# Projecting Q and K of the first two tiles from centred tokens, and scaling them afterwards on GpSimd

## The chip, the cores and the metric

The kernel runs on one core of a Trainium2 chip. The metric is the device time of one execution in microseconds (us); the smaller the better. Times of several runs are given as a median with the lowest and the highest.

## The reference

A block on 2048 tokens of 640 features, in bf16. The tokens are normalised (`_layernorm`, no weights), and two branches read the result: attention over a short dilated window, with 32 heads of 20 features, and a gated product of two linear layers. Both are added to the tokens.

```python
m = jnp.mean(x, -1); v = jnp.var(x, -1)
xn = (x - m) / jnp.sqrt(v + 1e-5)
q, k, v = (xn @ wqkv)                       # 640 x 1920, 32 heads of 20
idx = pos[:, None] - 2 * arange(8)[None]    # 8 keys, each second token back
attn = softmax(where(idx >= 0, q . k[idx] * 20 ** -0.5, -1e9))
A = (sum over w of attn * v[idx]) @ wo
B = ((xn @ w_gate) * (xn @ w_up)) @ w_down  # 640 -> 1536 -> 640
out = x + A + B
```

The deviation is one number for each token, so it may be divided out before or after the projection: `((x - m) * r) @ W` equals `((x - m) @ W) * r`.

## The kernel before

The tokens lie in 16 tiles of 128 (`XST`, one tile is 128 partitions by 640). For each tile, `front(t)` takes statistics on VectorE (two `bn_stats` of 320 columns at L579, `bn_aggr` at L582 into `MV`), the root of the variance on ScalarE (L589) and its reciprocal on VectorE (L596), both into `SD`, and then the normalised tokens `XNS`: on VectorE for tiles 0 to 5 (L608 in two pieces for tiles 0 and 1, L611 for the others), on ScalarE from tile 6 on (L614). The projections need the features on the partitions, so each tile is turned into `XNT`: tiles 0 to 3 by TensorE against an identity (L646) with a copy out of PSUM (L656, L658, L665), tiles 4 to 15 by a transposing DMA from SP's queue (L679).

Q and K of tiles 0 and 1 are projected by `proj_group` in `spread` (L734): for each chunk of 128 input features, five products of 128 by 128 into two neighbouring banks of PSUM, so that work can begin when the first chunks of the tokens and of the weights are there. ScalarE copies the result out (L707) into `QT` and `KT`. All other Q, K and V projections go by `mms` (L702). V of the first 512 tokens (`proj_v(0, m)`) needs tiles 0 to 3 in `XNT` and V's weights.

Before the first transposes, TensorE runs nine fillers of 512 columns on constants, and after tile 0's transposes three of 256 (`warm`, L686).

Behind the projections come: products of Q with shifted K on VectorE (`products`, L885 and L934), their sums by head on TensorE (L1017), softmax, the weighted V (L1196 on VectorE, L1201 on GpSimd, sums by head on TensorE at L1255), the gated layer (L1319) and the output projections (L1420, L1471).

The order on each engine is fixed when the program is built. `Sched.run` holds a list of tasks with priorities and estimated durations and times (`occ`, `land`), and picks the next one; at run time each engine goes through its list in order and waits for semaphores. Some instructions of VectorE and GpSimd carry `lock`: those of the one engine wait until those of the other, placed before them, are done. So an estimate that changes can move any instruction after it. The order of the first loads is written out by hand; the rest of SP's queue comes from `loads()`, in its order:

```python
x_half(0, 2.85)
x_half(1, 3.25, eng="act")
x_load(1, land=4.2)
wqkv_load(0, 0, 3, eng="act", land=5.5)
wqkv_load(1, 0, 2, land=6.4)
wqkv_load(0, 3, NCH, land=7.2)
x_load(2, land=7.6)
wqkv_load(1, 2, NCH, land=9.0)
```

After these, `loads()` issues tiles 3 to 11, V's weights in one transfer and tiles 12 to 15, each of these last once its place in `XST` is free.

Of the kernel before, what the change touches and what calls it, by code (L numbers as in the profile page):

```python
# [357 lines left out]
def build_kernel(nc, A_x, A_wqkv, A_wo, B_x, B_w_gate, B_w_up, B_w_down, out):  # L358
# [67 lines left out]
    QUAD = {2: (1, 0), 3: (1, 0)}  # L426
    LAST_DMA = ()
# [11 lines left out]
    MV = sb("MV", [128, NT, 2], FP32)  # L439
    SD = sb("SD", [128, NT, 4], FP32)  # L440
# [8 lines left out]
    vscr = nc.dram_tensor("v_scratch", [D, PAD + S], BF16, kind="Internal").ap()  # L449

# [53 lines left out]
    COPY = (("act", "act"), ("dve", "act"))  # L504
    STEPS = (((0, 2), (2, 3), (3, 4), (4, NCH)), ((0, 2), (2, 3), (3, NCH)))
# [19 lines left out]

    def loads():
        def t(f, *a):
            return Task("sp", lambda: f(*a), prio=0)

        for t_ in range(3, NXS):  # L530
            yield t(x_load, t_)
        yield t(wqkv_load, 2)
        for t_ in range(NXS, NT):
            yield have("apply", t_ - NXS)
            yield t(x_load, t_)

        def w(T, src):
            dma(T[:], src.rearrange("(c p) n -> p c n", p=128), w=[T[:]], name="ld_w")

        def pads():  # L540
            z = ZERO[:, 0:PAD].unsqueeze(1).to_broadcast([128, NCH, PAD])
            dma(vscr[:, 0:PAD].rearrange("(c p) s -> p c s", p=128), z, r=[ZERO[:, 0:PAD]], w=[("vscr", "pad")], name="vpad")

        yield have("xnt", NT - 1)
        yield t(w, WG, B_w_gate)
        yield t(pads)
        yield t(w, WU, B_w_up)

        def copy_x():
            a, b = ohbm[0:3 * JB, :], xhbm[0:3 * JB, :]  # L550
            o, i = a.rearrange("(p r) n -> p (r n)", p=128), b.rearrange("(p r) n -> p (r n)", p=128)
            op("sp", lambda e: e.dma_start(o, i), w=[("outx",)], dma=True, name="outx", nbytes=2e6)

        yield num(2, "lg")
        yield t(copy_x)
# [15 lines left out]
    def front(t):  # L571
        x, st = XST[:, xslot(t), :], STATS[:, t, 0:12]
        xs, mv = XNS[:, t % NXN, :], MV[:, t, 0:2]
        sd, rstd, nmr = SD[:, t, 0:1], SD[:, t, 1:2], SD[:, t, 2:3]
# [12 lines left out]
        def sqrt():  # L587
            o, i = SD[:, t0:t1, 0:1], MV[:, t0:t1, 1:2]
            op("act", lambda e: e.activation(o, i, ACT.Sqrt, bias=EPSC[:, 0:1]), r=[("mv", k) for k in ts] + [EPSC[:]],  # L589
               w=[("sd", k) for k in ts], name=f"sd{t}", occ=0.36)  # L590
            for k in ts:
                mark("sd", k)

        def recip():
            o, i = SD[:, t0:t1, 1:2], SD[:, t0:t1, 0:1]
            op("dve", lambda e: e.reciprocal(o, i), r=[("sd", k) for k in ts], w=[("rstd", k) for k in ts], name=f"rstd{t}", occ=0.16)  # L596
            if t >= N_DVE_A:
                n, m = SD[:, t0:t1, 2:3], MV[:, t0:t1, 0:1]
                op("dve", lambda e: e.scalar_tensor_tensor(n, m, -1.0, o, op0=ALU.mult, op1=ALU.mult),
                   r=[x for k in ts for x in (("mv", k), ("rstd", k))], w=[("nmr", k) for k in ts], name=f"nmr{t}", occ=0.13)  # L600
# [3 lines left out]
        def apply():  # L604
            if t < N_SPLIT:
                for a, b in [(128 * lo, 128 * hi) for lo, hi in PARTS[t]]:
                    o, i = XNS[:, t, a:b], x[:, a:b]
                    op("dve", (lambda o, i: lambda e: e.tensor_scalar(o, i, mv[:, 0:1], rstd, op0=ALU.subtract, op1=ALU.mult))(o, i),  # L608
                       r=[i, ("mv", t), ("rstd", t)], w=[o], name=f"lnap{t}", occ=0.09 + (b - a) * 0.55e-3)
            elif t < N_DVE_A:  # L610
                op("dve", lambda e: e.tensor_scalar(xs, x, mv[:, 0:1], rstd, op0=ALU.subtract, op1=ALU.mult),  # L611
                   r=[x, ("mv", t), ("rstd", t)], w=[xs], name=f"lnap{t}", occ=0.45)
# [6 lines left out]
        if t == 1:  # L619
            yield have("apply", 0)  # L620
        for i in range(2):
            if t == 2 and i == 0:
                yield have("apply", 1)
            if t == 2 and i == 1:
                yield have("xnt", t - 1)
# [11 lines left out]
        yield Task("dve" if t < N_DVE_A else "act", apply, r=[("rstd", t), x], w=[xs], prio=p)  # L637
        o = XNT[:, :, t * TS:(t + 1) * TS]
        if t < N_PE_T:
            hold = []  # L640

            def trans(k, *bs):
                hold.extend((b, PS[:, b, :].bitcast(BF16)[:, 0:NCH * 128].rearrange("p (c f) -> p c f", c=NCH)) for b in bs)
                for c in range(*PARTS[t][k]) if t < N_SPLIT else range(NCH):
                    i, q = xs[:, c * 128:(c + 1) * 128], hold[k][1][:, c, :]
                    op("pe", (lambda q, i: lambda e: e.transpose(q, i, IDENT[:]))(q, i), r=[i, IDENT[:]], w=[q],  # L646
                       name=f"tr{t}_{c}", occ=0.057, lat=0.2)
                if t == 0 and k:
                    warm(N_WARM)

            def part(k, eng):
                b, tpv = hold[k]
                lo, hi = PARTS[t][k]
                a, i = o[:, lo:hi], tpv[:, lo:hi]
                if eng == "dve":
                    X = op("dve", lambda e: e.tensor_copy(a, i), r=[PS[:, b, :]], w=[a], name=f"xntcp{t}_0", occ=0.1 + 0.08 * (hi - lo))  # L656
                else:
                    X = op("act", lambda e: e.activation(a, i, ACT.Copy), r=[PS[:, b, :]], w=[a], name=f"xntcp{t}_1",  # L658
                           occ=0.12 + 0.12 * (hi - lo))
                K.free_bank(b, X)  # L660
# [8 lines left out]

            if t < N_SPLIT:  # L670
                for k, ((lo, hi), e) in enumerate(zip(PARTS[t], COPY[t])):
                    yield Task("pe", (lambda k: lambda *bs: trans(k, *bs))(k), r=[xs[:, lo * 128:hi * 128]], prio=p, banks=1)
                    yield Task(e, (lambda k, e: lambda: part(k, e))(k, e), r=[PS[:, hold[k][0], :]], prio=p - 1)
            else:
                yield Task("pe", lambda b: trans(0, b), r=[xs], prio=p, banks=1)
                yield Task("dve" if t < N_DVE_C else "act", copy, r=[PS[:, hold[0][0], :]], prio=p)
        else:
# [3 lines left out]
            yield Task("sp", dmat, r=[xs], prio=1)  # L681
        mark("xnt", t)

# [36 lines left out]
    def proj_group(items, s0, n, prio, keys):  # L720
        hold = []

        def spread(k, *bs):
            which = items[0][0]
            if bs:
                p = PS[:, bs[0], :]
                p = bass.AP(p.tensor, p.offset, [p.ap[0], [n, NCH], [1, n]])
                hold.append((bs[0], [(qk_dst(which, 0, NCH, s0, n), p, NCH * n)]))
            b = hold[0][0]
            for c in range(*STEPS[s0 // TS][k]):  # L730
                for m in range(NCH):
                    o = PS[:, b + m // 4, m % 4 * n:m % 4 * n + n]
                    l, x = wcols(which, c, m), XNT[:, c, s0:s0 + n]
                    op("pe", (lambda o, l, x, c, m: lambda e: e.matmul(o, l, x, start=(c == 0 and m % 4 == 0), stop=(c == NCH - 1 and m >= 3)))(o, l, x, c, m),  # L734
                       r=[l, x], w=[o], name=f"p{which}_{s0}_{m}_{c}", occ=n / 2400 + 0.0024, lat=0.3)

# [10 lines left out]
        def ev():  # L747
            b, outs = hold[0]
            X = evac(outs, f"pev{items[0][0]}_{s0}")
            for i in range(2 if wide else 1):  # L750
                K.free_bank(b + i, X)
# [5 lines left out]
        wide = prio < 10  # L757
        if wide:
            for k, (lo, hi) in enumerate(STEPS[s0 // TS]):
                yield Task("pe", (lambda k: lambda *bs: spread(k, *bs))(k), r=[wcols(items[0][0], hi - 1, 0), XNT[:, hi - 1, s0:s0 + n]],  # L760
                           prio=prio, banks=0 if k else 2, contig=not k)
        else:
            yield Task("pe", go, r=[wcols(items[0][0], NCH - 1, 0), XNT[:, NCH - 1, s0 + n - TS:s0 + n]], prio=prio, banks=1)
        if wide:
            yield have("sd", 2 + items[0][0]) if s0 else have("xnt", 1)
        yield Task("act", ev, r=[o for _, o, _ in hold[0][1]], prio=5)

    def proj_qk():
        for pair in (0, 2):
            for t in (pair, pair + 1):  # L770
                yield have("xnt", t)
                for which in (0, 1):
                    K.spawn(proj_group([(which, 0, 4 if pair else 5)], t * TS, TS, 10 if pair else FIRST + 0.5 * which + 0.2 * t, None))
            if pair:
                for which in (0, 1):
                    K.spawn(proj_group([(which, 4, 1)], pair * TS, 2 * TS, 10.2, None))
# [12 lines left out]
    def proj_v(j, m):  # L789
# [15 lines left out]
        yield Task("pe", go, r=[WQKV[:, WPOS[2], 4, 0:64], XNT[:, NCH - 1, j * JB:(j + 1) * JB]], prio=30 + j, banks=1)  # L805
# [12 lines left out]
    free = list(range(NPR - 1))  # L818
# [693 lines left out]
    GROUPS = ((4, 5), (6, 7), (8, 9), (10, 11), (12, 13), (14, 15))  # L1512
    N_DVE_A = 6
    N_DVE_C = 5
    N_SPLIT = 2
    N_WARM = 3
# [9 lines left out]
    x_half(0, 2.85)  # L1526
    x_half(1, 3.25, eng="act")
    x_load(1, land=4.2)
    wqkv_load(0, 0, 3, eng="act", land=5.5)
    wqkv_load(1, 0, 2, land=6.4)  # L1530
    wqkv_load(0, 3, NCH, land=7.2)
    x_load(2, land=7.6)
    wqkv_load(1, 2, NCH, land=9.0)
    K.t["act"] = 2.95
# [10 lines left out]

    K.spawn(loads())
    for t in range(NT):
        K.spawn(front(t))
    K.spawn(proj_qk())
# [50 lines left out]
```

## Time and profile before

| | us |
|---|---|
| median of 3 runs | 264.64 (264.5 to 264.82) |
| the profiled execution | 264.51 |
| its span, first to last instruction | 262.8 |

| engine | busy us | share of the span | instructions |
|---|---|---|---|
| PE (TensorE matmul) | 259.3 | 99% | 1586 |
| DVE (VectorE) | 219.0 | 83% | 259 |
| POOL (GpSimd) | 160.5 | 61% | 97 |
| ACT (ScalarE) | 112.7 | 43% | 198 |

The profile shows one execution, in us from its first instruction. Its page gives the busy time of each engine, the chain of waits that ended last, the costliest groups of instructions (line, engine, operation, output<-inputs) and the transfers with the time from issue to landing. The trace behind it can be asked for the same in any stretch of time, for one line or one tile, and for who waited for whom. SP and ACT issue most transfers; a "q" behind an engine's name marks its sequencer.

### The profile page before, as it was taken

What the parts mean: (1) busy time and instruction counts of PE and PEld (TensorE: products, weight loads), DVE (VectorE), ACT (ScalarE), POOL (GpSimd) and SP (SyncE); (2) the same over time, 40 slices, a digit from 0 to 9 for tenths busy, and PEclk for the clock granted to TensorE, in tenths of its full rate; (3) what the DMA queues carried; (4) which work ended last, traced back from release to release, by engine and by line L of the source; (5) the groups of instructions that cost most, each with busy time, mean ns of one, the idle gap of its engine ahead of it and who ended that gap; (6) DMA issues with size and microseconds to landing.
All of it is one profiled execution on the core that took longest, in us unless ns stands there. A gap on an engine that the chain in (4) does not pass through costs nothing.

```text
span 262.8 us, 4098 instructions
## 1 busy us (share of the span) xinstructions
PE 259.3 (99%) x1586; PEld 135.7 (52%) x1586; DVE 219.0 (83%) x259; ACT 112.7 (43%) x198; POOL 160.5 (61%) x97
## 2 busy tenths in 40 slices
PE   8999999999999999999999999999999999999996
PEld 3986964444444444444444444444444444445675
DVE  4888899999897897868779899999989989995041
ACT  3559987546522121224267665451324116211300
POOL 3000000000699999899983465899979999999300
PEclk9999999999999999999999999999999999999999
DMA  7996699932489996640349702666679766821621
GB/s 222 365 216 106 119 183 386 336 152 100 127 153 190 248 207 118 118 87 1 80 118 302 171 7 50 142 131 174 148 181 199 189 140 143 140 60 37 91 65 50
DMA packets 47891, 39.77 MB, mean 151 GB/s; under 512 B 23776, under 2 KB 45536, under 8 KB 47840
## 3 DMA queue, kind: packets, MB, share of 16 engines
q1 hardware_dynamic: 44448, 32.72, 48.3%
q0 software_dynamic: 2736, 6.16, 13.8%
q10 hardware_dynamic: 688, 0.64, 0.7%
q8 instruction: 12, 0.20, 0.3%
q14 instruction: 7, 0.06, 0.1%
HBM read 25.07 MB, written 7.23 MB: 123 GB/s over the span
## 4 chain that ended last, share of the span: by engine, by line
PE 97%; DMA 1%; DVE 1%; ACT 0%; issue 0%
PE PS L1319 40%; PE PS L702 23%; PE PS L1420 21%; PE PS L1471 7%; PE PS L734 2%; PE PS L1017 2%; PE PS L1255 2%; DMA XST<-in_A_x_dram 1%; PE PS L646 1%; DVE STATS L579 0%; DVE XNS L608 0%; PE PS L686 0%; ACT SD L589 0%; DVE FB L1484 0%; DVE MV L582 0%
## 5 line engine op out<-in xcount | busy, mean ns | idle before, releaser
L1201 POOL TENSOR_TENSOR SV<-PV 128x1024 bf16<-128x1024 f32 x40 | 94.1, 2523 | 17.8 <-DVE SM L1050 4.2
L1196 DVE TENSOR_TENSOR PV<-VX,PS 128x1024 f32<-128x1024 bf16 (+1 forms) x54 | 90.7, 1730 | 2.8 <-POOL SV L1201 2.8
L702 PE MATMUL PS<-XNT,WQKV 128*128 128x512 bf16 (+2 forms) x390 | 60.7, 316 | 0.0
L1319 PE MATMUL PS<-XNT,WG 128*128 128x512 bf16 x240 | 59.7, 379 | 0.0
L1319 PE MATMUL PS<-XNT,WU 128*128 128x512 bf16 x240 | 59.6, 379 | 0.0
L702 PEld LDWEIGHTS PS<-XNT,WQKV 128*128 128x128 bf16 x390 | 37.8, 112 | 21.9 <-ACT LOG L1028 0.8
L934 DVE TENSOR_TENSOR PRF<-PS,KT 128x1024 f32<-128x1024 f32 x32 | 38.0, 1217 | 0.3 <-PE PS L702 0.3
L1319 PEld LDWEIGHTS PS<-XNT,WG 128*128 128x128 bf16 x240 | 23.3, 98 | 28.7 <-DVE XNT L1328 0.4
L1319 PEld LDWEIGHTS PS<-XNT,WU 128*128 128x128 bf16 x240 | 23.5, 98 | 28.3
L960 POOL TENSOR_TENSOR PRF<-PRF,PRF 128x1024 f32<-128x1024 f32 x8 | 21.0, 2629 | 21.6 <-DVE LOG L1077 21.6
L707 ACT ACTIVATE HT<-PS 128x512 bf16<-128x512 f32 x24 | 14.4, 598 | 35.4 <-PE PS L1319 35.4
L1420 PE MATMUL PS<-HT,WD 128*128 128x512 bf16 x120 | 27.5, 379 | 0.0
L885 DVE TENSOR_TENSOR PRD<-QT,KT 128x2048 bf16<-128x2048 bf16 x24 | 27.5, 1217 | 0.0
L707 ACT ACTIVATE UX<-PS 128x512 bf16<-128x512 f32 x15 | 9.0, 597 | 41.6 <-PE PS L1420 41.6
L1036 POOL MEMSET LOG<- 32x6 bf16 (+6 forms) x7 | 0.4, 95 | 42.1 <-ACT LOG L1028 42.1
L993 POOL TENSOR_TENSOR PRD<-PRF,PRF 128x1024 bf16<-128x1024 f32 x8 | 20.6, 2625 | 0.1
L971 POOL TENSOR_TENSOR PRF<-PRF,PRD 128x1024 f32<-128x1024 f32 x8 | 19.7, 2564 | 0.0
L1420 PEld LDWEIGHTS PS<-HT,WD 128*128 128x128 bf16 x120 | 11.6, 98 | 14.4 <-ACT OT L1264 0.4
L1420 PE MATMUL PS<-OT,WO 128*128 128x512 bf16 x75 | 18.6, 379 | 0.0
L1328 DVE TENSOR_TENSOR HT<-HT,PS 128x512 bf16<-128x512 bf16 x18 | 12.3, 684 | 7.2 <-PE PS L1319 7.1
L1484 DVE TENSOR_TENSOR FB<-PS,XR 128x320 bf16<-128x320 f32 (+2 forms) x9 | 4.1, 455 | 16.2 <-PE PS L1471 15.2
L579 DVE BATCH_NORM_STATS2 STATS<-XST 128x6 f32<-128x320 bf16 x32 | 14.2, 467 | 1.9 <-DMA XST<-in_A_x_dram 1.9
(76 smaller groups left out, 247.0 us busy)
## 6 DMA issues: line engine op xcount, KB each, us to landing
VX<-v_scratch SPq DMA_DIRECT2D x80, 130.0 KB, 3.1
PRF<-PRF POOLq DMA_DIRECT2D x8, 512.0 KB, 5.4
v_scratch<-VST SPq DMA_DIRECT2D x4, 640.0 KB, 6.1
XST<-in_A_x_dram SPq DMA_DIRECT2D x15, 160.0 KB, 5.6
WG<-in_B_w_gate_dram SPq DMA_DIRECT2D x1, 1920.0 KB, 9.0
WU<-in_B_w_up_dram SPq DMA_DIRECT2D x1, 1920.0 KB, 12.5
out_dram<-in_A_x_dram SPq DMA_DIRECT2D x1, 1920.0 KB, 17.9
WD<-in_B_w_down_dram SPq DMA_DIRECT2D x1, 1920.0 KB, 8.7
```

The lines of the kernel that those rows point to most:

```text
L702: op("pe", (lambda o, l, x, c, first: lambda e: e.matmul(o, l, x, start=first, stop=(c == NCH - 1)))(o, l, x, c, first), r=[l, x], w=[o], ...
L707: X = op("act", (lambda o, i: lambda e: e.activation(o, i, ACT.Copy))(o, i), r=[i], w=[o], name=name, occ=0.12 + n * 0.9e-3)
L885: op("dve", lambda e: e.tensor_tensor(s[:], qb, kv, ALU.mult), r=[q, rk], w=[s[:]], name=f"prod{j}_{r}_{c}", occ=1.15, lock=True)
L934: X = op("dve", lambda e: e.tensor_tensor(o[:], qb, kv, ALU.mult), r=[q, rk, ("qev", j, c)], w=[o[:]], name=f"prow{j}_{r}_{c}_{q0}", occ=1.17)
L960: yield Task("pool", lambda: op("pool", lambda e: e.tensor_tensor(x, x, y, ALU.add), r=[x, y] + tokens(), w=[x], name=name, occ=2.36, lock ...
L971: yield Task("pool", lambda: op("pool", lambda e: e.tensor_tensor(x, x, z, ALU.add), r=[x, z] + tokens(), w=[x], name=name + "c", occ=2.36 ...
L993: yield Task("pool", lambda: op("pool", lambda e: e.tensor_tensor(o, a, y, ALU.add), r=[a, y] + tokens(), w=[o], name=f"qend{j}_{r}_{q0}", ...
L1196: last[0] = op("dve", lambda e: e.tensor_tensor(p, vw, a, ALU.mult), r=[vv] + rk, w=[p], name=f"pv{u}_{x}_{r0}", occ=0.09 + 1.1 * nr)
L1201: X = op("pool", lambda e: e.tensor_tensor(o, p[:, :, 0, :], p[:, :, 1, :], ALU.add), r=[p[:]] + tokens(), w=[o], name=f"pva{u}_{x}", occ= ...
L1319: op("pe", (lambda l, x, c: lambda e: e.matmul(PS[:, b, :], l, x, start=(c == 0), stop=(c == NCH - 1)))(l, x, c), r=[l, x], w=[PS[:, b, :] ...
L1420: op("pe", (lambda l, x, i: lambda e: e.matmul(PS[:, b, :], l, x, start=(i == 0), stop=(i == n - 1)))(l, x, i), r=[l, x], w=[PS[:, b, :]], ...
L1471: op("pe", (lambda l, x, i: lambda e: e.matmul(dst, l, x, start=(i == 0), stop=(i == n - 1)))(l, x, i), r=[l, x], w=[PS[:, b, :]], name=f" ...
```

## The change

For tiles 0 and 1, a new thread `raw(t)` subtracts only the mean (`XCT`): tile 0 on VectorE with the mean of `bn_aggr`, tile 1 on ScalarE with a mean that ScalarE sums itself (`xsum`). TensorE turns these centred tokens, VectorE copies them to `XRAW`, and `raw_group` projects Q and K from them, chunk by chunk, into PSUM; ScalarE copies the results as fp32 to `RAW`. The reciprocal deviations of both tiles are stored to a scratch in DRAM and loaded again along the free dimension on all partitions (`ROWS`), and GpSimd multiplies, four times 128 by 640 (`rsc`). Statistics' root and reciprocal are taken for tiles 0 and 1 together; they are normalised too, later, by VectorE, and turned by a transposing DMA, since V and the gated layer read `XNT`. ScalarE's program has a second load of a function table, between tile 1's centring and the first root.

Q's weights and K's are loaded in chunks of 128 input features, Q's from two queues in turn; V's in two parts of columns. After K's weights the order on SP's queue is: the store of the reciprocals (which waits for them), tiles 4 to 6, the load of the rows (which waits for the store), the transposes of tiles 0 and 1 (each waits for the normalised tile), V's weights 0 to 255, tile 7, V's weights 256 to 639, tiles 8 to 11, and then as before. The list of free places for products begins with others (the first ones are taken by the new tiles), and the planner puts five more wide projections ahead of the first sums by head.

On TensorE the order is now: tile 0's transposes, fillers, Q of tile 0 (25 products), tile 1's transposes, 55 products of K and Q of tiles 0 and 1, tile 2's transposes, the 20 products left, and tile 2's and 3's work as before.

```diff
+    RAW = K.sbuf("RAW", [128, 2, 2, NCH, TS], FP32, a_wd)
+    XRAW = K.sbuf("XRAW", [128, NCH, 2 * TS], BF16, a_wd + 3 * 4096)
+    XCT = K.sbuf("XCT", [128, 2, D], BF16, a_pr)
+    XSUM = K.sbuf("XSUM", [128, D], FP32, a_pr + 4096)
+    ROWS = K.sbuf("ROWS", [128, 2 * TS, 2], FP32, a_wd + 4 * 4096)
...
     def loads():
...
-        for t_ in range(3, NXS):
-            yield t(x_load, t_)
-        yield t(wqkv_load, 2)
+        yield have("rstd", 1)
+        yield Task("sp", row_store, r=[("rstd", 1)], prio=0)
+        for t_ in range(4, 7):
+            yield t(x_load, t_, "sp", lands[t_])
+        yield Task("sp", row_load, r=[("rscr",)], prio=0)
+        for k in range(N_RAW):
+            yield have("xs", k)
+            mark("dtr", k)
+            yield have("xnt", k)
+        yield t(wv_load, 0, 256, 15.1)
+        yield t(x_load, 7, "sp", lands[7])
+        yield t(wv_load, 256, D, 16.6)
+        for t_ in range(8, NXS):
+            yield t(x_load, t_, "sp", lands[t_])
+        yield have("xnt", 5)
...
+    def raw(t):
...
+        def total():
+            op("act", lambda e: e.activation(XSUM[:], x, ACT.Copy, scale=-1.0 / D, accum_out=mean), ...)
...
+            if CENTRE[t] == "dve":
+                op("dve", lambda e: e.tensor_scalar(o, i, mean, None, op0=ALU.subtract), ...)
+            else:
+                op("act", lambda e: e.activation(o, i, ACT.Identity, bias=mean), ...)
...
+    def norm(which, t):
+        yield have("raw", which, t)
+        yield have("rows")
+        yield have("apply", 5)
...
+            op("pool", lambda e: e.tensor_tensor(d, x, rs, ALU.mult), ..., lock=True)
...
-    free = list(range(NPR - 1))
+    free = [6, 7, 8, 9, 10, 3, 4, 0, 1, 2, 5]
...
-    GROUPS = ((4, 5), (6, 7), (8, 9), (10, 11), (12, 13), (14, 15))
+    GROUPS = ((0, 1), (4, 5), (6, 7), (8, 9), (10, 11), (12, 13), (14, 15))
...
-    x_half(0, 2.85)
+    x_half(0, 3.05)
     x_half(1, 3.25, eng="act")
-    x_load(1, land=4.2)
-    wqkv_load(0, 0, 3, eng="act", land=5.5)
...
+    x_load(1, eng="act", land=3.9)
+    wqkv_load(0, 0, 1, land=4.5)
+    wqkv_load(0, 1, 2, eng="act", land=4.9)
+    wqkv_load(0, 2, 3, land=5.3)
+    wqkv_load(0, 3, 4, eng="act", land=5.7)
+    wqkv_load(0, 4, NCH, land=6.1)
+    wqkv_load(1, 0, 1, land=6.5)
+    x_load(2, land=6.95)
+    wqkv_load(1, 1, 2, land=7.4)
+    wqkv_load(1, 2, 3, land=7.8)
+    wqkv_load(1, 3, 4, land=8.2)
+    x_load(3, land=8.65)
+    wqkv_load(1, 4, NCH, land=9.1)
```

## The prediction

> **What bounds the kernel now.** I read the chain that ended last first, then who waits on TensorE (PE), then the first 14 us of that chain in order of time.
>
> ```profile
> PE 97%; DMA 1%; DVE 1%; ACT 0%; issue 0%
> ```
> ```profile
> PE PS L686 <- PEq L1585: 0.9, 1, 0.9
> PE PS L646 <- DVE XNS L608: 0.3, 1, 0.3
> ```
> PE is the path. After its first transposes it never waits again, so the time is "when useful PE work starts" plus a fixed amount of PE work plus any wait that the change adds. The start:
>
> ```profile
> 0.82 2.25 DMA XST<-in_A_x_dram
> ...
> 3.10 0.90 DVE STATS L579 x2
> ...
> 4.02 0.22 DVE MV L582
> ...
> 4.26 0.30 ACT SD L589
> ...
> 4.59 0.17 DVE SD L596
> ...
> 4.79 0.35 DVE XNS L608
> ...
> 5.19 0.29 PE PS L646 x2
> 5.48 0.00 issue
> 5.48 0.34 PE PS L646 x3
> 5.82 0.33 PE PS L686 x3
> 6.15 1.40 PE PS L734 x25
> ```
> The change takes the square root and reciprocal (4.26 to 4.79) out of this chain. What it adds lies on ScalarE (ACT), on SP's queue and in the landings of loads, for which I read the timeline, the DMA view and the page's queue rows:
>
> ```profile
> 39.95 0.60 ACT L707 ACTIVATE QT<-PS 128x512 bf16<-128x512 f32 x1 [0.48 <-PE PS L702]
> 40.56 1.28 ACT L1541 ACT_TABLE_LOAD   x1
> 41.86 1.08 ACT L707 ACTIVATE KT<-PS 128x512 bf16<-128x512 f32 x2
> ```
> ```profile
> L679 SPq DMA_TRANSPOSE XNT<-XNS x12: 1199/1274/2644, 16.4 to 33.2; - x12
> ```
> ```profile
> q8 instruction: 12, 0.20, 0.3%
> ```
> A table switch costs 1.3 us of ACT. A DMA transpose holds SP for 1.2 to 1.3 us, the first one for 2.64. The instruction queue moves 12 packets of 16 KB; its packet records show the first two at 13.39 (1.11 us long) and 17.26 (1.40 us). Each holds one DMA engine: the 800 KB V weights, at the rate of the loads around them (160 KB per 0.44 us: XST landings 10.23, 10.67, 11.12 ...), were due 2.2 us after 13.36 and landed at 16.76, 1.2 late; the transpose issued at 16.44 landed after 3.75 us, against 2.6 for most.
>
> **The change part by part.** Sums are against the profiled execution, 264.51 us (span 262.8, 1.7 around it), 0.13 below the median 264.64; I add the differences to the median.
>
> *Start, −0.54.* Aggregation ends at 4.23, so the centring pieces run at 4.26 and 4.52 (0.35, 0.37, the L608 rows). The last three transposes start at 4.95, not 5.48; three fillers follow as before; the first projection moves from 5.99 to 5.45. The copies out of PSUM go to VectorE (DVE): 0.29 for two chunks (L656), 0.37 for three (between that and 0.49 for five), ending 5.27 and 5.69; chunk 2 is needed at 5.45 + 10 × 0.056 = 6.01. Amounts of PE work stay: 20 transposes, 12 fillers, the same projections.
>
> *Weights by chunk, 0 to +0.3, taken 0.* By bytes in order of issue at 160 KB per 0.44 us from 320 KB at 4.40, Q's chunks land at 4.85, two by 5.7, two by 6.6; they are needed at 5.45, 5.73, 6.01, 6.29, 6.57. K's come last at 9.7 and are needed at 10.7. A wait here eats into the next one rather than adding to it.
>
> *Tile 1 on ACT, tile 2 behind it, 0 to +0.6, taken +0.1.* Tile 1 lands 4.4 to 4.85 (4.40 before). ACT then sums it (0.70 to 0.91, the 640-element rows L707 and L614), centres two pieces (0.38 to 0.51, 0.49 to 0.62, the L658 rows and the same with 0.13 of SBUF and pointer cost from L614), ending near 6.4, loads the square root's table (1.28) to 7.75 and takes the root (0.30) to 8.05. DVE stands in order behind it: reciprocal, two statistics, aggregation, root, reciprocal, tile 2's normalisation. In the trace that string takes 2.25 us from L579 at 7.97 to L646 at 10.21, so tile 2 is ready at 8.09 + 0.08 + 2.2 = 10.4. PE gets there after 25 + 5 + 55 instructions of 0.056 and two changeovers: 10.25.
>
> *Normalised tiles 0, 1 for V.* DVE gains two normalisations (0.45 each, L611) and three copies, loses 0.64 of tile 1's: about +1.2. DVE had 2.9 us of waits for the root's reciprocals in the front, so its products move by a microsecond or so; the first logits stand 45 and not 40 wide projections after the rest, +1.08 of cover: 0. If the cover is gone, it's that microsecond.
>
> *SP's queue, 0 to +2.0, taken +0.45.* Here work is moved. After the K load SP waits for the reciprocal, stores rows, loads x4 to x6, waits about 2 us for the store (ATX landings 1.9), loads the rows, waits for normalised tiles 0 and 1 (near 11.9 and 12.9), issues two transposes, and only then V's weights and x7 to x11, which in the kernel before were issued by 8.4. With 1.25 us a transpose the first V part (320 KB) is issued at 14.45 and lands at 17.0 to 17.3 (x loads: first data about 1 us after issue, 0.88 of data, 0.4 to 0.75 to landing); PE wants it at 17.5 (18.04 before, less 0.54). The second part (480 KB, behind x7) would land at 19.0, wanted at 17.5 + 10 × 0.216 = 19.7. But the second instruction packet stands 0.78 us ahead of V in PE's order (17.26 against 18.04), so near 16.8, and holds one engine to about 18.1; that engine then has 1.7 us of x7 and V left: 19.8, landed 20.2. Hence +0.45 between 0 and 0.7. If the first transpose takes 2.64 here too, everything behind moves by 1.4: the second rival.
>
> *GpSimd's four scalings, 0.* 2523 ns × 640/1024 = 1.6 us each, from tile 5's normalisation (17.6) to 24.1, the row transfer long landed. Who waits: DVE's first product, 29.57 before. Cover 5 us.
>
> *Later stages, 0.* Product slots are dealt out in another order; PE's amounts are equal. The tightest later cover is the last sums: GpSimd ends at 244.16, PE starts L1255 at 245.50.
>
> Sum: −0.54 + 0.1 + 0.45 = 0.0, so 264.6.
>
> **Two rules against the change.** The row of the table load above shows ACT running again 0.02 us after 1.28 us of loading, with nothing lost ahead of it. The Trainium skill, "ScalarE: Activation LUTs", section "What ACT_TABLE_LOAD costs", counts a drain of about 1.38 us besides, 2.66 in all; by an estimate from that page tile 2 would be ready 1.4 us later. This trace disagrees.
> The nine fillers run at 427 ns for 512 columns, the transposes at 5.19 follow each other at 56 ns for 128: the full rate came between 4.65 and 5.19 (the granted-clock record: 4.76). Work that starts at 4.7 has no margin. The Trainium skill, "TensorE: Matmul & The Clock Gate", section on the HAM clock gate, says the window that decides is free-running, so the change of rate may come later in another run; the three times of before, within 0.32 us, speak against much of that.
>
> **The rivals.**
> 1. *All hidden* (chance 0.17). V's weights and tile 2 come in time: 264.64 − 0.54 = 264.1. For it: every margin I gave is only a few tenths. Against: the loads behind the transposes.
> 2. *V's weights become the path* (0.30). If the first transpose holds SP for 2.64 us as in the trace, V's first part is issued at 15.85, lands at 18.7 free, 19.6 if the instruction packet holds one engine; PE, in order, waits 1.2 to 2.0: 265.3 to 266.1. It decides as soon as the landing passes 18.0, where the gain is gone. For: that row. Against: the long one was issued 0.8 us before the packet at 17.26, with an earlier load still queued on that engine; the transpose at 33.24, with a packet at 34.14, held SP 1.28 us. So it may be the packet, not being first.
> 3. *ACT stands still after the second table load* (0.06). If it stood as long again as the load's 1.28 us, tile 2 would be ready at 11.7, PE would wait 1.4 there, and V, wanted 1.4 later, no more: 264.64 − 0.54 + 1.4 = 265.5. It decides once tile 2 passes 10.8. Against: the row of the load before, which shows no such pause. (The page on ScalarE above has one.)
> 4. *The half rate reaches useful work* (0.05): the change of rate a microsecond later than 4.76 costs half of what stands in it, 0.5 us, of which tile 2's wait takes back 0.1: 264.6 + 0.4 = 265.0.
>
> **How the numbers follow.** The forecast has chance 0.42: 264.6, its own range 264.2 to 265.0. The range for all, 264.0 to 266.0, leaves out the best tenth (all hidden and the margin of a run) and the worst tenth (rival 2 with the packet on the first part). A measurement of this kernel tells about 0.2%, 0.53 us, from no change. Faster by more: rival 1 sits at the edge with −0.54, most of it, and a little of the forecast: 0.17. Slower by more: rivals 2 and 3 in full, little else: 0.38. The same: 0.45.
>
> **What would show it.** Right: the first projection starting near 5.45; a second table load on ACT between 6 and 8; tile 2's transposes at 10.3 to 10.5; a PE wait of some tenths on the V weights between 17 and 20; from there on PE without waits and products starting a microsecond later. Wrong: PE waits in the V projections over 1 us (rival 2), no wait there (rival 1), tile 2's transposes past 10.8 (rival 3), projections at 112 ns near 5 us (rival 4), or any PE wait after 43 us, which I have at nothing.

## The result and the profile after

The changed kernel takes 268.29 us (median of 6 runs, 266.6 to 270.12) against 264.62 (264.45 to 264.82) for the kernel before, run beside it: a ratio of 1.0144, 95% interval 1.0098 to 1.019, so it is 1.4% slower. The profiled execution took 268.67, its span is 266.9 (262.8 before). Forecast were 264.6 and at most 266.0.

The engines of the chain of waits that ended last, and who kept PE waiting (us in total, times, longest), after the change:

```profile
PE 89%; DMA 8%; DVE 1%; SPq 0%; ACTq 0%; issue 0%
...
PE PS L829 <- DMA WQKV<-in_A_wqkv_dram: 1.1, 1, 1.1
PE PS L829 <- DMA XNT<-XNS: 1.1, 1, 1.1
PE PS L829 <- DVE XNT L664: 1.0, 1, 1.0
...
PE PS L755 <- DMA WQKV<-in_A_wqkv_dram: 0.6, 1, 0.6
```

PE was 97% of the chain and is 89%; DMA has gone from 1% to 8%. Four new waits stand on PE, 3.8 us together. The chain in order of time (start, length, what) shows where:

```profile
1.75 4.51 DMA WQKV<-in_A_wqkv_dram
...
8.58 0.39 SPq L486
...
9.01 6.20 DMA XST<-in_A_x_dram
...
15.23 0.49 DVE STATS L600
15.73 0.39 DVE XNT L664
...
21.72 5.74 DMA XNT<-XNS
...
27.51 20.82 PE PS L829 x145
```

From 27.51 on PE is the chain again, as before. So the whole loss lies ahead of it: the projections of tiles 4 and 5, which start here, started at 23.44 before (+4.07; the span is +4.1).

| start on PE, us | before | after | difference |
|---|---|---|---|
| first projection | 5.99 | 5.29 | −0.70 |
| first wide projections (tile 2) | 12.20 | 12.49 | +0.29 |
| V's first projection | 18.04 | 20.83 | +2.79 |
| projections of tiles 4 and 5 | 23.44 | 27.51 | +4.07 |

The start is 0.70 earlier, and already gone at 12.49: Q's second chunk, issued from ACT's queue, landed at 6.25 (0.57 of wait), and shorter waits of this kind follow. Then tile 4 takes 6.20 from issue to landing. DVE takes its instructions in order: it stands at tile 4's statistics with tile 3's copy (15.73) behind them, and PE waits for that copy until 16.18 (1.01). V's first weights are issued at 16.81 and land at 20.79 (1.14 of wait); tile 5, normalised at 19.52, is transposed from 21.72 on, when SP comes to it, behind tiles 8 to 11 in the queue, and lands at 27.46 (1.07). Counted from one start of a PE instruction to the next, these three waits cost 1.20, 1.31 and 1.27 us, 3.78 together, a little more than their idle time. So the sum closes: 0.70 gained at the start, 0.99 lost up to 12.49, 3.78 lost in the three waits make +4.07.

What is behind the 6.20? The next view cuts the profile after into stretches of 1 us. Each row has busy time and number of instructions of PE, PEld (loads of TensorE's weights), DVE, ACT and POOL, then PE's granted clock, the busy share of the 16 DMA engines (a packet counts whole where it starts, so it can exceed 1) and, last, GB/s:

```profile
8.00:9.00 1.00, 1.00 (x19) 0.91 (x18) 1.00 (x5) 0.55 (x1) 0.00 (x0) 1.00 0.95 343
9.00:10.00 1.00, 1.00 (x22) 1.00 (x20) 0.93 (x3) 0.39 (x2) 0.00 (x0) 1.00 0.22 28
10.00:11.00 1.00, 1.00 (x22) 1.00 (x20) 0.96 (x4) 0.61 (x1) 0.00 (x0) 1.00 1.55 46
11.00:12.00 1.00, 1.00 (x22) 1.00 (x20) 0.48 (x3) 0.00 (x0) 0.00 (x0) 1.00 0.34 74
12.00:13.00 1.00, 1.00 (x22) 1.00 (x20) 0.91 (x5) 0.78 (x2) 0.00 (x0) 1.00 0.25 45
13.00:14.00 1.00, 1.00 (x21) 1.00 (x20) 0.55 (x2) 0.89 (x3) 0.00 (x0) 1.00 0.41 23
```

The loads run at 343 GB/s from 8 to 9. At 8.58 the store of the reciprocals is issued: 2 KB in 256 pieces of 8 bytes. For five microseconds after, the core moves 23 to 74 GB/s, although tiles 4 to 6 are queued from 9.0 to 10.0 on. The DMA view has the store's time from issue to landing, 4.5 (last number of a row):

```profile
ATX<-LOG SPq DMA_DIRECT2D x32, 32.0 KB, 2.0
...
row_scratch<-MV SPq DMA_DIRECT2D x1, 2.0 KB, 4.5
```

### The profile page after: what moved, and what is told of

Its sections match the earlier page's. It is cut to its first block, busy times and chain, and to the rows that moved or that the text cites. A ratio compares the mean times of both kernels' runs of the same rounds, so it can differ in the third digit from the quotient of the medians.

```text
span 266.9 us, 4115 instructions
## 1 busy us (share of the span) xinstructions
PE 260.0 (97%) x1586; PEld 135.7 (51%) x1586; DVE 220.0 (82%) x261; ACT 114.4 (43%) x199; POOL 166.5 (62%) x101
## 4 chain that ended last, share of the span: by engine, by line
PE 89%; DMA 8%; DVE 1%; SPq 0%; ACTq 0%; issue 0%
PE PS L1421 39%; PE PS L1522 21%; PE PS L829 18%; PE PS L1573 7%; DMA XST<-in_A_x_dram 4%; DMA XNT<-XNS 2%; PE PS L1119 2%; PE PS L1357 2%; DMA WQKV<-in_A_wqkv_dram 2%; PE PS L755 1%; DVE STATS L600 1%; SPq L486 0%; ACTq L486 0%; DVE XRAW L714 0%; DVE XNT L664 0%
## 5 line engine op out<-in xcount | busy, mean ns | idle before, releaser
L829 PE MATMUL PS<-XNT,WQKV 128*128 128x512 bf16 (+2 forms) x390 | 61.4, 316 | 3.2 <-DMA WQKV<-in_A_wqkv_dram 1.1
L829 PEld LDWEIGHTS PS<-XNT,WQKV 128*128 128x128 bf16 x390 | 37.7, 113 | 25.9 <-DMA WQKV<-in_A_wqkv_dram 1.7
## 6 DMA issues: line engine op xcount, KB each, us to landing
out_dram<-in_A_x_dram SPq DMA_DIRECT2D x1, 1920.0 KB, 17.9
```

What stands on the lines that cost most here:

```text
L829: op("pe", (lambda o, l, x, c, first: lambda e: e.matmul(o, l, x, start=first, stop=(c == NCH - 1)))(o, l, x, c, first), r=[l, x], w=[o], ...
```

## The experiments

Theory S: the store itself holds what is queued behind it. Theory O: the order of SP's queue (V's weights behind rows and transposes) costs the time. Theory C: loading Q and K by chunks costs what it was to gain. All medians are compared with the kernel before, run beside them (264.54 for the first four kernels, 264.64 for the next four, 264.66 and 264.64 for the last two pairs).

**Without the rows.**

```diff
-        yield have("rstd", 1)
-        yield Task("sp", row_store, r=[("rstd", 1)], prio=0)
+        yield Task("pool", row_ones, prio=0)          # ROWS filled with 1
...
-        yield Task("sp", row_load, r=[("rscr",)], prio=0)
```

> Leaves out the store and the load of the reciprocal deviations (GpSimd fills the rows with ones, so Q and K of tiles 0 and 1 stay unscaled); all else as in the changed kernel. Theory S (the store of 256 pieces of 8 bytes holds the DMA engines for about 4 us, and all behind it on SP's queue): tiles 4 to 6 are issued near 6.0 and land by 11.5, the 1.2 us PE wait for tile 3's copy is gone, V's weights are issued 0.5 to 1 us earlier onto free engines; total 264.9 to 266.0. Rival O (the order on SP's queue, V's weights and tiles 7 to 11 behind two transposes, costs the time; the store is harmless): PE waits of about 1.1 us each for V's weights and for tile 5's transpose stay, 266.5 to 267.5.

Measured: 267.22 (266.54 to 268.15), ratio 1.0101 (1.0076 to 1.0126). Tiles 4 to 6 land from 10.16 to 10.97 and the wait at tile 3 is gone. What is left on PE in the profile is V alone, at both its parts:

```profile
PE PS L831 <- DMA WQKV<-in_A_wqkv_dram: 1.3, 2, 1.0
```

V's second part is issued at 16.12 and lands at 21.78, with an instruction packet of 1.23 us at 18.18. So most of the loss, 2.7 of 3.7 us, stays without the store. The time is in the range of rival O; tile 5's transpose, which O also named, is not waited for. C is left in this kernel too, though in this profile PE waits for no chunk of Q.

**The store from ACT's queue.** `eng="act"` for the store and its wait.

> The same store, issued from ScalarE's queue instead of SP's, with no other change; SP goes on with tiles 4 to 6 near 6.0. If the store holds the DMA engines themselves (S), the data of tiles 4 to 6 still in flight at 8.6 is held and they land at 13 or later, with PE waiting for tile 3's copy as before: 267 to 268. If it only holds the queue that it stands in (S'), they land at 10.5 to 11.4 and that wait is gone: 266.0 to 266.8. Rival O: the waits for V's weights and tile 5's transpose stay in either case.

Measured: 267.83 (267.53 to 268.6), 1.013 (1.0109 to 1.0151). The store takes 4.3 again (8.5 to 12.78); tiles 4 to 6, now in another queue, land at 11.53 to 12.58, and not at 15.2 to 17.4. Against the 10.2 to 11.0 without a store they are still 1.4 to 1.6 late, but that is not shown to be the store's doing: K's first chunk landed at 8.52, 1.5 late (7.02 without a store), and the store was issued only at 8.50. So this run shows a hold on the store's own queue, and at most 0.2 us on the other. The landings are those of neither forecast. The time lies where S had it, but for other waits: PE's gain at tile 3 is spent on 0.87 for that chunk of K and 1.24 for V's second part.

**Tiles 4 to 6 ahead of the store.** The three loads change places with the store.

> Tiles 4 to 6 are issued on SP's queue ahead of the store, with no other change. S: they land at 10.5 to 11.4, PE's wait for tile 3's copy (about 1.2 us) goes away; the store lands as late as before, so the rows, the transposes and V's weights are as late as before and PE waits longer for V (2 us or more): the total falls by less than 1.2, to 267.0 to 268.0. O says the same of V and gives 267 to 268 too; the landings are what counts here.

Measured: 267.18 (267.02 to 268.9), 1.0112 (1.008 to 1.0144), in the range expected. Tiles 4 to 6 land at 10.45 to 11.26 and tile 3's wait is gone; V's first part costs 1.44 in its place, its second 0.45.

**All loads first.** Tiles 4 to 6, V's two parts with tile 7 between them, tiles 8 to 11, the transposes, then the store and the rows.

> On SP's queue: tiles 4 to 6, V's weights, tiles 7 to 11, then the two transposes, then the store and the load of the rows; no other change. Both S and O: every PE wait but that for Q's first weight chunks is gone, and the early start is kept less about 0.8 us of those waits: 264.4 to 265.0. Against both: if the late store now holds the transposes of tiles 4 to 7 or the rows come after 24 us, waits of 1 us or more appear behind V: 265.5 or more.

Measured: 266.67 (266.18 to 267.0), 1.0076 (1.0061 to 1.0091): the branch "against both". PE does not wait for V any more. It waits for the transpose of tile 5: SP stood until 20.34 for the store (issued 15.8), and only then issued the rows and the transposes.

```profile
PE PS L829 <- DMA XNT<-XNS: 1.4, 1, 1.4
...
PE PS L755 <- DMA WQKV<-in_A_wqkv_dram: 0.5, 1, 0.5
```

**The store alone, in the kernel before.** One transfer is added to the kernel before, between tile 3's load and tile 4's, behind both tiles' statistics; nothing else changes. First 256 pieces of 8 bytes, then two rows of 1 KB.

```diff
-        for t_ in range(3, NXS):
+        yield t(x_load, 3)
+        yield have("mv", 1)
+        yield t(probe)       # rscr[t, p, :] <- MV[p, t, 0:2]; or rscr <- ZERO[0:2, :]
+        for t_ in range(4, NXS):
```

> The kernel before with one more transfer and nothing else: 128 partitions by 2 tiles by 8 bytes of MV go to a scratch in DRAM from SP's queue, between tile 3's load and tile 4's (2 KB in 256 pieces of 8 bytes; it waits for both tiles' statistics). Theory S (such a store takes 4 us and more, and what is queued behind it on SP lands late): tile 4, 10.23 in the profile of before, lands at 12.5 or later, V's weights (16.76) at 18.5 or later, and PE, which wants V's weights at 18.04, waits: 265.2 to 267.5. Rival O (only the order of the queue cost the time, the store is harmless): V's weights later by the wait for the statistics and one issue, under 0.6 us: 264.6 (within 0.3).

> The same, but the 2 KB are two rows of 1 KB of zeros (2 pieces), at the same place in the queue and behind the same statistics. Theory S with the size of the pieces as the cause: the store lands about 2 us after its issue, tile 4 and V's weights land at most 0.8 us later than in the kernel before: 264.6 (within 0.3), and at least 0.6 below the kernel with 256 pieces. If any store there holds the queue (the direction and not the pieces): as slow as that kernel.

Measured: 266.18 (265.63 to 266.66), 1.0058 (1.004 to 1.0077), with the small pieces; 264.59 (264.52 to 264.77), 0.9999 (0.9989 to 1.0008), with the two rows. The same 2 KB, from the same place in the queue. The rows of the waits of the first, and the windows of the first and then of the second:

```profile
PE PS L711 <- DMA WQKV<-in_A_wqkv_dram: 1.7, 1, 1.7
```
```profile
9.00:10.00 1.00, 1.00 (x22) 1.00 (x20) 0.55 (x3) 0.59 (x3) 0.00 (x0) 1.00 1.55 355
10.00:11.00 1.00, 1.00 (x22) 1.00 (x20) 0.83 (x3) 0.66 (x1) 0.00 (x0) 1.00 0.91 109
11.00:12.00 1.00, 1.00 (x22) 1.00 (x20) 0.97 (x4) 0.73 (x2) 0.00 (x0) 1.00 0.86 113
```
```profile
9.00:10.00 1.00, 1.00 (x22) 1.00 (x20) 0.55 (x3) 0.59 (x3) 0.00 (x0) 1.00 1.09 330
10.00:11.00 1.00, 1.00 (x22) 1.00 (x20) 0.83 (x3) 0.61 (x1) 0.00 (x0) 1.00 1.00 355
11.00:12.00 1.00, 1.00 (x22) 1.00 (x20) 0.96 (x4) 0.79 (x2) 0.00 (x0) 1.00 1.09 329
```

With small pieces the rate falls from 355 to 109 GB/s while the DMA engines count as busy; with two rows it stays at 329 and more in these stretches. The store with small pieces landed 5.2 us after its issue, tile 4 at 11.88 where it was 10.23, V's weights at 19.74 where they were 16.76; in the kernel with two rows V's weights landed at 17.85 and PE did not wait. One part of the expectation failed: tile 4 landed at 11.88, not at 12.5 or later, 0.2 after the store. The queue does not stand meanwhile, it goes on slowly. S is shown: the same 2 KB cost 1.5 us in 256 pieces of 8 bytes and nothing in two of 1 KB. The size and the number of the pieces changed together, and so did the partitions that they are read from; which of these counts was not tested.

The Trainium skill, "DMA: Bandwidth & Descriptors", gives 512 bytes in its "Specifications" as the least size for full rate and has the engine read, modify and write below it; its section "Why small descriptors are slow (HBM only)" spares transfers from SBUF to SBUF. The times here agree with both, though they do not show the mechanism: the store of 8-byte pieces to DRAM lands after 3.7 to 5.2 in the nine profiles that have it, the `ATX` transfers inside SBUF, in pieces of 256 bytes, after 2.0.

**Q's chunks from one queue.** Chunks 1 and 3 move from ACT's queue to SP's, between their neighbours.

> The changed kernel with Q's weight chunks 1 and 3 issued on SP's queue between its neighbours, and not from ACT's: all five chunks of Q come in order on one queue. In the profile of the changed kernel chunk 1 landed after chunk 2 and chunk 3 after chunk 4, with PE waits of 0.57 and some 0.2 at 6.3 to 7.0. Theory C (two queues side by side deliver the chunks out of order): chunk 1 lands by 5.6, chunk 3 by 6.5, the wait falls under 0.25, tile 2's transposes start 0.3 to 0.6 earlier than 11.10. V's weights stay late by the same clock time (issue behind the store and the transposes), so the gain is eaten there: 268.0 (within 1 of the changed kernel). Rival (the rate of all loads is the bound there, not their order): the wait stays at 0.5 and more.

Measured: 269.57 (267.69 to 271.05), 1.0184 (1.0123 to 1.0245). Chunk 1 lands at 4.81 and chunk 3 at 6.84, and the first wait falls to 0.11. But chunk 2 landed at 6.40, behind a stretch (5.0 to 5.5) in which the loads moved 182 GB/s, the last chunk at 7.31 (6.97 in the changed kernel), and tile 2's transposes start at 11.16, not earlier than 11.10. Expected was a gain of 0.3 to 0.6 there and a time within 1 of the changed kernel: both missed, though the intervals of the two ratios overlap. The chunks now come in order, and it gained nothing. That the wait is shorter is not the order's doing alone: the first projection started at 5.70, 0.41 later than in the changed kernel.

**Late rows.** Q's chunks as in the last kernel; SP's queue as in "all loads first", but the store ahead of the transposes of tiles 4 and 5 and the rows behind them.

> The changed kernel with Q's chunks all on SP in order, and SP's queue after K's weights in this order: tiles 4 to 6, V's weights and tiles 7 to 11, the transposes of tiles 0 and 1, the store of the reciprocals, the transposes of tiles 4 and 5, and only then the rows. Against the kernel with V first but the rows ahead of tile 4's transpose (266.67, where PE waited 0.49 for Q's chunk and 1.38 for tile 5's transpose): theory S + O + C says both waits go and 1.6 to 1.9 with them: 264.9, that is level with before to 0.5 above. If the 1.38 comes from the store's pieces holding the transposes behind it in the queue and not from SP waiting for the store, tile 5's transpose is still late by about 1: 265.9. Rival (the rest of the loss lies in the other form of the early stage itself): 266.2 to 266.7.

Measured: 265.98 (265.45 to 266.7), 1.0061 (1.0041 to 1.0081). The forecast of 264.9 missed. The number is that of the second branch, 265.9, but not its cause: the wait for tile 5's transpose is gone. Left in the profile (its execution: 265.45) are 0.23 for Q's last chunk and 0.42 for tile 1's transpose, which landed at 18.70 behind tile 11.

**The transposes ahead of tiles 8 to 11; then the grouped weights.** The first of two kernels moves the transposes of tiles 0 and 1 in front of those loads. The second, in addition, loads Q's and K's weights in the four groups of the kernel before:

```diff
-    x_load(1, eng="act", land=3.9)
-    wqkv_load(0, 0, 1, land=4.5)
...
+    x_load(1, land=3.9)
+    wqkv_load(0, 0, 3, eng="act", land=4.5)
+    wqkv_load(0, 3, NCH, land=5.7)
+    wqkv_load(1, 0, 2, land=6.5)
     x_load(2, land=6.95)
+    wqkv_load(1, 2, NCH, land=9.1)
```

> The kernel with the late rows, but the transposes of tiles 0 and 1 are issued ahead of tiles 8 to 11 (behind V's two parts and tile 7). There PE waited 0.42 at 18.97 for tile 1's transpose (landed 18.70, queued behind tile 11's 17.45) and 0.23 at 7.36 for Q's last chunk. Theory: with 2.2 MB less in front of it tile 1's transpose lands by 17.8, PE wants it near 18.5 and does not wait; 0.4 less than that kernel: 265.5, still above before by the chunks' wait. Rival (it is the transpose's own issue at 14.1 and an instruction packet that make it late, not the loads ahead): no change, 266.0.

> The same queue, but the weights of Q and K are loaded in the four groups of the kernel before (Q's chunks 0 to 2 from ACT's queue, tile 1 from SP's) and not chunk by chunk. In the kernels with chunks the loads moved 177 to 330 GB/s in parts of 3.5 to 6.5 us, against 358 to 392 in the kernel before, and every one of them had a PE wait of 0.1 to 0.7 for a chunk of Q. Theory (the chunks cost what they were to gain): Q's first three chunks land by 5.6, the last two by 6.7, first projection 5.4 to 5.85, no PE wait over 0.25 before 12 us, the first 20 wide projections (12.20 before) start at 11.7 to 12.0: 264.3, level with before or 0.3 below. Rival (the centred form itself costs something that the chunks hide): 264.9 and more, as the kernel with chunks.

Measured: 266.03 (264.96 to 267.49), 1.0051 (1.0028 to 1.0073), and 266.12 (264.84 to 267.53), 1.0048 (1.0026 to 1.0071). In the first tile 1's transpose lands at 17.24 and its wait is gone, as the theory said, but tile 5's is back (0.37 at 24.43) and another follows (0.46 at 30.55), so the 265.5 missed. In the second the first wide projections start at 12.16, against 12.67 in the first (12.25 to 13.25 in all profiles with chunks), and no wait for weights is left in PE's rows. So far the theory of the chunks held, though 11.7 to 12.0 was forecast. But the time did not move:

```profile
PE PS L829 <- DMA XNT<-XNS: 1.8, 2, 1.1
```

The transposes of tiles 5 and 7 stand behind the store (17.9 to 22.94) and tiles 8 to 11. The forecast of 264.3 for this kernel missed by 1.8 in the median, and this row is 1.8 in its profiled execution (266.73).

**The same without the store, and with the rows made on the engines.** The first kernel fills the rows with ones; the second computes everything, without a DMA for the rows (the three operations, written short):

```diff
+    DIAG[:, t, :] = activation(IDENT, ACT.Copy, scale=MV[:, t, 0:1])     # ScalarE, t = 0, 1
+    PS[:, b, 0:256] = matmul(ones 128x128, DIAG)                          # TensorE, once
+    ROWS[:, :, 0] = activation(PS[:, b, 0:256], ACT.Copy)                 # ScalarE
```

> The kernel with the grouped weights (median 266.12, its profiled execution 266.73), without the store and the load of the rows: GpSimd fills the rows with ones, so Q and K of tiles 0 and 1 stay unscaled (that part of the computation is left out). In the profile of the grouped kernel the first 20 wide projections start at 12.16 (12.20 before), and PE then waits 1.13 and 0.70 for the DMA transposes of tiles 5 and 7, which stand behind the store (17.9>22.94) and tiles 8 to 11. Theory S: without the store both waits go, 1.8 with them: 264.7 to 264.9, level with before, and less when the full rate of PE comes early. Rival (the transposes are late because tiles 8 to 11 and two instruction packets stand in front of them, the store adds nothing): 266.0 and more.

> The whole computation again, the same as the kernel with ones, but the rows come without any DMA: ScalarE multiplies the identity by the reciprocal deviations (two of 128 by 128), TensorE sums it with ones (one product of 256 columns, 0.11), ScalarE copies the result out of PSUM. Theory S + O + C (the store, the order of the queue and the chunks were the whole loss): as the kernel with ones, plus 0.1: 264.8, within 0.3 of before, and 3 us below the changed kernel. Rival (something else of the centred form costs time later): 265.5 and more, with waits of PE after 28 us.

Measured: 264.66 (264.35 to 264.94), 0.9994 (0.9984 to 1.0004), and 264.88 (264.49 to 266.09), 1.0011 (0.9998 to 1.0025). With ones, no wait of PE for a load or a transpose is left; the rows of its waits begin:

```profile
PE PS L815 <- PEq L1700: 0.9, 1, 0.9
PE PS L831 <- issue: 0.3, 2, 0.2
```

With S, O and C undone together the centred form is level with the kernel before, and 3.4 us below the changed kernel, so the three account for the loss, to within the interval. Neither kernel is faster than before. The profile of the one that computes everything is of a slower execution, 265.80, and still has a wait for tile 5's transpose, which landed at 24.65 behind tiles 8 to 11:

```profile
PE PS L854 <- DMA XNT<-XNS: 0.8, 1, 0.8
```

So the queue's order is not wholly put right there, even without a store. In the profile with ones the first projection starts at 5.62 (5.99 before), the first wide ones at 12.07 (12.20), the end is 0.1 earlier. Of an earlier start of 0.37, 0.24 is lost before 12.07: 0.16 in front of tile 2's transposes, the rest at changes between sets of products. For the kernel that computes everything the interval leaves open whether it is level or a little slower.

## Why the prediction was wrong

**The step that failed is SP's queue, "0 to +2.0, taken +0.45".** The term was mis-sized: the three waits that hang on this queue measured 3.2 us of PE's idle time, 3.8 from start to start. The first price that failed is the store's: it went by `ATX`, about 2 us, and the store took 4.5, and its neighbours in the queue paid. By that price the load of the rows would have gone out near 10.6 (8.58 + 2); it went out at 13.09. Tile 0 was normalised at 12.49, not 11.9, and its transpose went out behind the rows, at 13.46. The second transpose held SP for 1.95, not 1.25. So V's first part, forecast for 14.45, went out at 16.81. The second price that failed is V's landing, taken from the first loads of tokens: 2.55 to 2.85 after the issue. It took 3.98, to 20.79.

The store is therefore not the whole of it. Without it V's first part went out at 14.93 and still took 3.57, the second part landed at 21.78, not at 20.2, and PE waited 1.25 for the two where 0.45 was taken. Why V's weights landed so slowly there, behind two transposes and beside an instruction packet, stays open.

The nearest row for the store's price was not used. `ATX` (1.9 in the kernel before) goes from SBUF to SBUF. The DMA view of the kernel before also has a store to DRAM in small pieces, of 640 times 28 bytes:

```profile
v_scratch<-ZERO SPq DMA_DIRECT2D x1, 17.5 KB, 8.6
```

It does not give 4.5, since a good part of its 8.6 is a queue of other transfers (its pieces run from 41.77 on, after an issue at 35.6). But it would have put the upper bound of the store well above 2, and the queue behind it among the things to be priced.

**Two more waits were not seen.** The prediction followed SP's queue only up to V. It counted tile 4's load as moved, but not who stands behind it on DVE: the statistics of tile 4 are ahead of tile 3's copy (1.01). And V was not the end of the queue: tiles 8 to 11 and the transposes behind them were late too (1.07).

**Weights by chunk, "taken 0", measured some 0.9**: Q's first 25 products and what PE waits between them take 2.32 us (5.29 to 7.61), and 1.40 in the kernel with ones (5.62 to 7.02). By bytes in order of issue the chunks would have come in time; from two queues they came out of order (chunk 2 at 5.92, chunk 1 at 6.25), and the loads ran at 274 to 333 GB/s up to 6, against 358 to 392 before. The two kernels that differ only in how these first loads are cut and queued show 12.16 against 12.67, but the same time, since later waits took it up. The size changes from run to run: without the rows the same chunks came at 346 to 379 GB/s, and PE waited for none of Q's.

**The start, "−0.54", was right in its mechanism** and measured −0.70: first projection at 5.29, forecast 5.45. Part of that is luck, since PE's full rate came early in this execution; in others of these kernels it started at 5.6 to 5.8 (last section). **Tile 2, "ready at 10.4"**, was ready at 10.66, and PE, itself late, got there at 11.10 without a wait. **GpSimd's scalings, 0**, took 1.6 us each, from 19.6 to 25.9, and nobody waited. **Later stages, 0**: right, the order of PE behind 27.51 shows no new wait.

**The rivals.** Rival 1, all hidden, is out with the first of the waits. Rival 2, V's weights as the path, named the place of one of the three large waits, with a wrong cause: the first transpose did not take 2.64 but 1.3 of SP's time (13.46 to 14.8). It is the second one that held SP until 16.76, with an instruction packet of 0.96 us at 14.74: "the packet, not being first" was right. In the kernel without rows, with no packet beside them, the two took 1.30 and 1.27. Rival 3 did not happen. The timeline of ScalarE shows the second table load and the root 0.01 us behind its end:

```profile
6.37 1.28 ACT L610 ACT_TABLE_LOAD   x1
7.66 0.30 ACT L610 ACTIVATE MV<-MV,EPSC 128x2 f32<-128x2 f32 x1
```

Rival 4, half rate in useful work, had a chance of 0.05. It did not come in this profile, but it came in others (last section).

**The chances.** With 0.45 on "the same" and an upper end of 266.0, the range counted one wait on one term. A queue that carries everything behind it shifts every later transfer on it, and the bound should have been the sum of the waits that this can cause.

## What to carry to other kernels

A transfer's size says little about its price: look at its pieces and where they go, and price it by a row of the same kind. When a slow or waiting transfer enters a queue, list all that stands behind it to the queue's end, and for each who waits for it, on engines that run in order too. A few values that must change from one axis to the other went cheaper here over TensorE (one product of 256 columns, three short operations of ScalarE: 264.88) than by way of DRAM (266.12 in the kernel that differs in this alone).

## What the runs showed of the hardware

Pieces of 8 bytes do not look expensive in the record: the 256 of the changed kernel ran from 9.49 to 9.73, 9 ns each. What is slow are the 1280-byte packets behind them: 177 of them start between 9.5 and 14.5 us, where 268 started from 8 to 9 alone. Most still take 55 ns, single ones up to 3.8 us.

The moment at which PE's rate doubles differs from run to run. At half rate a transpose takes 107 ns and a filler of 256 columns 213, at full rate 56 and 113. Two timelines, of the changed kernel and of the one with late rows:

```profile
4.55 0.57 PE L705 MATMUL PS<-IDENT,XCT 128*128 128x128 bf16 x5
4.96 0.49 PE L813 MATMUL PS<-const-bfloat16-1.0 128*128 128x256 bf16 x3
```
```profile
4.65 0.74 PE L705 MATMUL PS<-IDENT,XCT 128*128 128x128 bf16 x5
5.18 0.83 PE L813 MATMUL PS<-const-bfloat16-1.0 128*128 128x256 bf16 x3
```

In the profiles of the eleven kernels with centred tokens the change came between 3.75 and 4.8 in five and between 5.3 and 6.5 in six, with the same nine fillers from 0.86 on. A late one puts the first projection of the kernels with chunks at 5.6 to 5.8 instead of 5.3. The Trainium skill, "TensorE: Matmul & The Clock Gate", section on the HAM clock gate, calls the window that decides free-running and has the moment vary by 500 ns from run to run. The profiles agree that it moves, but by more, some 2.7 us. What starts ahead of that change runs at half rate, so part of an earlier start is worth half of itself: here in six profiles of eleven.
